# An mLSTM cell and a gelu feed-forward on one core: masks, two weight transfers, first states and idle products moved

## The chip, the cores and the metric

The kernel runs on one core of a Trainium2 chip. A core has TensorE (PE: products and, by a product with an identity, transposes), VectorE (DVE), ScalarE (ACT), GpSimd (POOL) and SyncE (SP), whose queue here issues every transfer. PEld is TensorE's loading of weights, which overlaps its products. The metric is the time of one execution in microseconds (us) on the device; lower is better.

## The reference

Two stages, all in float32. The first is an mLSTM cell over 4 batches, 8 heads, 768 steps and head size 40. It is a recurrence:

```python
for t in range(S):
    kt, vt, qt = (k[:, :, t], v[:, :, t], q[:, :, t])
    m_new = np.maximum(f_gate[:, :, t] + m, i_gate[:, :, t])
    f_stab = np.exp(f_gate[:, :, t] + m - m_new)
    i_stab = np.exp(i_gate[:, :, t] - m_new)
    m = m_new
    C = f_stab[:, :, None, None] * C + i_stab[:, :, None, None] * np.einsum('bhd,bhe->bhde', vt, kt)
    n = f_stab[:, :, None] * n + i_stab[:, :, None] * kt
    h_tilde = np.einsum('bhde,bhe->bhd', C, qt)
    nq = np.einsum('bhd,bhd->bh', n, qt)[:, :, None]
    denom = np.maximum(np.abs(nq), 1.0)
    o = 1.0 / (1.0 + np.exp(-o_gate[:, :, t]))
    y[:, :, t] = o * h_tilde / denom
```

The second stage takes the heads side by side as x (3072 tokens by 320) and computes

```python
h = x @ w_in                              # 320 x 2048
g = h * (1.0 / (1.0 + np.exp(-1.702 * h)))
return (g @ w_out).astype(np.float32)     # 2048 x 320
```

## The kernel before

The 768 steps are cut into six chunks `w` of 128 steps. A chunk is turned from a recurrence into products: scores of keys with queries, weighted by gates, times the values, plus what a carried state adds. Then the chunk's 512 tokens (4 batches of 128 steps) go through the feed-forward: up (320 to 2048), gelu, down (2048 to 320). While the feed-forward of chunk `w` runs on TensorE, the attention of chunk `w + 1` is laid in between its blocks.

Instructions stand on each engine in the order in which the program writes them; that order is made by hand. Tiles are taken from pools with a fixed number of buffers, and waits between engines come from who reads and writes which tile.

The first chunk has nothing to be laid beside, so it runs alone at the start. The parts that matter here:

- Transfers. SyncE issues, in this order: the gates of chunk 0; key and query of batch b for b = 0 to 3, with one weight piece behind each of b = 1, 2, 3; value and output gate of each batch; weight pieces 3 to 9. The weights are fetched as raw 32-bit pairs (two words per value) in pieces of 512 columns, and each piece is turned into the kernel's weight format by `convert` (L233 to L244): two operations of ScalarE, then four of VectorE. w_in has 320 rows: pieces of its first 128 and next 128 rows (`piece_in`, L132), and pieces 2 and 7 (`piece_rest`, L136) of the last 64 rows. A rest piece holds eight blocks of 128 columns, four in the upper and four in the lower 64 partitions, and `fetch` (L157) loads it with eight transfers of 64 KB.
- Idle products. `keep_busy(n)` (L186) issues n bf16 products of a tile of zeros into a PSUM bank that nothing reads. Eight stand at the start, four after `columns(0)`, two after each batch's values.
- Constants. After the identity, VectorE makes `pick`, then the masks `swap` and `keep` with the help of `odd` (L211 to L214), then `par`, `pair`, `half`. The masks are read only by `columns(w)` for w of 1 and more (L313, L314). Behind the constants in VectorE's queue stand the gates of chunk 0.
- `gates(0)` (L247): two scans along the steps and the sums around them on VectorE. GpSimd splits one of the results into three bf16 parts (`a3`, L261 to L264), VectorE another (`m3`, L272 to L275). They feed the products L367 and L368 in `weights(0, b)`, which build the exponents of the gate weights.
- For each batch: transposes of key and query (L338, copied out by ScalarE), scores (L387), weights (L363 to L368), with conversions of pieces 0 and 1 in between. Then for each batch tanh of the output gate (L731), values (L429), `outputs` on VectorE (L408 to L417) with a small copy of GpSimd (L420), idle products, and one batch later the `seam`: three transposes (L463) and a copy by ScalarE (L465), which put the batch's result into `xT`. The fourth seam stands alone at the end.
- The first feed-forward begins with `up(0, 0)` (L502): L512 multiplies the 256 first rows of w_in with `xT`, L518 the last 64. Between the blocks of `up` stand the products of the first carried state (`carry(0, c)`, L482, products at L490, copied to `state` by VectorE at L494) and conversions of the next pieces; after the fourth, `gates(1)` on VectorE.

Of the kernel before, what the change touches and what calls it, by code (L numbers as in the profile page):

```python
# [12 lines left out]
OP = mybir.AluOpType  # L13
AX = mybir.AxisListType
# [12 lines left out]
def kernel(  # L27
# [12 lines left out]
    nc = tc.nc  # L40
    B, H, S, D = q.shape
    BH = B * H
# [21 lines left out]
    op = ctx.enter_context(tc.tile_pool(name="op", bufs=2))  # L64
# [5 lines left out]
    V, A, G, T = nc.vector, nc.scalar, nc.gpsimd, nc.tensor  # L70
# [26 lines left out]
    def k_cols(w, t, h):  # L97

        return k_of(w)[t, h, :] if w < 2 else k_st[t, h * D:h * D + DP]
# [26 lines left out]
    rest_bits = w_in_bits[256:DM, :].rearrange("k (j two m) -> two k j m", two=2, m=256)  # L126
# [8 lines left out]

    def piece_rest(n):  # L136
        return (w_in_x[:, n * 4:n * 4 + 4, :].rearrange("p j m -> p (j m)"),
                [(slice(i * 64, i * 64 + 64), slice(j * 128, j * 128 + 128), rest_bits[i][:, n * 4 + j, :])
                 for i in range(2) for j in range(4)])

    def piece_out(n):
        parts, c = [], n * 512
# [12 lines left out]
    bits = {}  # L155

    def fetch(n):  # L157
        if n < 3 or 10 <= n < 13:
            bits[n] = s_in[:, n % 10].rearrange("p j m -> p (j m)").bitcast(U32).rearrange("p (a two) -> p a two", two=2)
        elif n == 17:  # L160
            bits[n] = t_flat[:, at_bits:at_bits + 1024].bitcast(U32).rearrange("p (a two) -> p a two", two=2)
        else:
            bits[n] = (gp if 6 <= n < 10 else sp).tile([128, 512, 2], U32, tag="g", name="bits")
        for r, c, src in pieces[n][1]:
            nc.sync.dma_start(out=bits[n][r, c].rearrange("p a two -> p (a two)"), in_=src)  # L165

    wt = {(0, b): gp.tile([L, NP, 2, L], FP, tag="g", name="wt") for b in range(B)}
    load_gates(0)
# [17 lines left out]
    def keep_busy(n):  # L186
        for _ in range(n):
            T.matmul(p_idle, idle, idle.unsqueeze(1).to_broadcast([128, 4, 128]), start=True, stop=True)
# [15 lines left out]
    for j in range(3):  # L204
        V.tensor_scalar(out=pick[j * BH:(j + 1) * BH, :], in0=ident[0:BH, 0:BH], scalar1=-1.0, scalar2=None,
                        op0=OP.mult)

    keep, swap = (const.tile([3 * BH, 3 * BH], FP, name=n) for n in ("keep", "swap"))
    odd = const.tile([3 * BH, 1], FP, name="odd")
    full = ident[0:3 * BH, 0:3 * BH]  # L210
    V.tensor_reduce(out=odd, in_=full.rearrange("p (j two) -> p two j", two=2)[:, 1], axis=AX.X, op=OP.add)  # L211
    V.tensor_scalar(out=swap, in0=full, scalar1=odd, scalar2=None, op0=OP.mult)
    V.memset(swap[BH:2 * BH, :], 0.0)
    V.tensor_tensor(out=keep, in0=full, in1=swap, op=OP.subtract)  # L214

    half = const.tile([BH, 2, 64], FP, name="half")
    par = const.tile([BH, 2], FP, name="par")
# [7 lines left out]
    state = [const.tile([128, BH // 2, D1], FP, name=f"state{i}") for i in range(2)]  # L225
# [76 lines left out]
    def slot(i, x):  # L302

        return slice((x ^ i) * HL, (x ^ i) * HL + HL)

    def banks(name):
        return ps_a.tile([128, 2, 512], FP, tag="a", name=name)

    def columns(w):
        pt = banks("p_cols")[:, 0, :]  # L310
        st = stacked[w]
        if w:
            T.matmul(pt[:, 0:3 * BH], st[0], keep, start=True, stop=False)  # L313
            T.matmul(pt[:, 0:3 * BH], st[1], swap, start=False, stop=True)  # L314
        else:
            T.transpose(pt[:, 0:3 * BH], st, full)
        n = 3 * BH
        if w in dec:
            n += BH
            T.matmul(pt[:, 3 * BH:n], half.rearrange("p a b -> p (a b)"), dec[w].rearrange("p a b -> p (a b)"),  # L320
                     start=True, stop=True)
        c = cols[w] = gate.tile([L, 4 * BH], FP, name="cols")
        V.tensor_copy(out=c[:, 0:BH], in_=pt[:, 0:BH])
        A.activation(out=c[:, BH:3 * BH], in_=pt[:, BH:3 * BH], func=AF.Exp, scale=-1.0)
        if w in dec:
            A.activation(out=c[:, 3 * BH:n], in_=pt[:, 3 * BH:n], func=AF.Exp)
# [130 lines left out]
    def seam(w, c, bs=(0, 1)):  # L457
        if w not in xT:
            xT[w] = work.tile([128, 3, B, L], FP, tag="xT", bufs=1, name="xT")
        px = banks("p_x")[:, 0:len(bs), 0:3 * L]  # L460
        for n, b in enumerate(bs):
            for x in range(3):
                T.transpose(px[:, n, x * L:(x + 1) * L], ys[w, c][:, b, x * 128:(x + 1) * 128], ident)  # L463
        b = 2 * c + bs[0]
        A.copy(out=xT[w][:, :, b:b + len(bs), :].rearrange("r x b t -> r b x t"),  # L465
               in_=px.rearrange("r b (x t) -> r b x t", t=L))
# [15 lines left out]
    def carry(w, c):  # L482
        js = slice(c * NJ, (c + 1) * NJ)
        pc = banks("p_c")
        n = 2 if 0 < w < NW - 1 else 1
        for j in range(NJ):
            for i in range(2):
                for x in range(n):
                    t = slot(i, x) if w else slice(0, L)
                    T.matmul(pc[i * 64:i * 64 + 64, x, j * D1:(j + 1) * D1], k_cols(w, t, c * PH + 2 * j + i),  # L490
                             vw[w, c][t, 2 * j + i, :], start=True, stop=True)
        new = lambda x: pc[:, x, 0:NJ * D1].rearrange("r (j d) -> r j d", d=D1)
        if w == 0:
            V.tensor_copy(out=state[1][:, js], in_=new(0))  # L494
            return
        for x, dst in enumerate((state_mid, state[1 - w % 2])[:n]):
            if x:
                decay(w, c, x, V)
            V.tensor_tensor(out=dst[:, js], in0=new(x), in1=dst[:, js], op=OP.add)
# [204 lines left out]
    def run(calls):  # L704
        for f, *args in calls:
            f(*args)
# [21 lines left out]
    for b in range(B + 1):  # L728
        if b < B:
            hs = slice(b * H, (b + 1) * H)  # L730
            A.activation(out=eo[0][:, hs, :], in_=eo[0][:, hs, :], func=AF.Tanh, scale=0.5)  # L731
            values(0, b)
            if b == 1:
                convert(2)
            keep_busy(2)
        if b:
            seam(0, (b - 1) // 2, ((b - 1) % 2,))


    beside = [((3, 4), (10, 11, 12, 13, 14)), ((5, 6, 7), (15,)), ((8, 9, 10), (16,)), ((11, 12, 13), (17, 18, 19)),  # L740
# [2 lines left out]
    def weights_in(n):  # L743
        for p in beside[n][0]:
            convert(p)
        for p in beside[n][1]:
            fetch(p)
# [8 lines left out]
    for w in range(NW):  # L756
        more = w + 1 < NW
        if w == 0:
            for j in range(NF // 2):
                if j % 2 == 0:  # L760
                    weights_in(j // 2)
                    up(w, j)
                if j == 0:
                    load(1, "o")
                if j < B:
                    (carry if j % 2 else scale)(0, j // 2)
                if j == 3:
                    gates(1)
                if j == 4:
                    load(1, "v")  # L770
                    spread(1)
                if j >= B:
                    transposes(1, j - B)
        else:
            token_sums(w)
            if more:
                gates(w + 1)
                load(w + 1, "o")
            for j in range(NF // 2):
                up_fast(w, j)  # L780
                if w == 1 and j < 4:
                    weight_sums(j)
                if more and j == 2:
                    load(w + 1, "vk")
                    spread(w + 1)
                if more and j:
                    for n in ((), (0, 2), (4,), (6, 1), (3,), (5, 7), ())[j - 1]:
                        block_transposes(w + 1, n)
                if j in (6, 7):
                    for late in (False, True):  # L790
                        hidden_sums(w, j - 6, late)
            gelu_fast(w, NF // 2 - 1)
            run([(hidden_sums, w, j, False) for j in (2, 3)])
        side = attention(w + 1) if more else {}
        if w == 0:

            blocks = [(lambda b=b, n=n: down(w, b, n)) for n0 in (0, 2) for b in range(B) for n in (n0, n0 + 1)]
        else:
            blocks = down_fast(w, 0) + down_fast(w, 1)
        for i, block in enumerate(blocks):  # L800
            if w == 0 and i < 6:
                weights_in(4 + i)
            if w + 2 < NW and i == (6 if w == 0 else 0):
                load_gates(w + 2)
            if w + 2 < NW and i == 13:
                load_squares(w + 2)
            block()
            run(side.get(i, []))
            if w and i == 0:
                run([(hidden_sums, w, j, True) for j in (2, 3)])  # L810
            if w == 0 and i in (11, 14):
                input_sums(slice(0, 4) if i == 11 else slice(4, 8))
# [30 lines left out]
```

## Time and profile before

| | us |
|---|---|
| median of 3 runs | 487.61 (487.58 to 489.2) |
| the profiled execution, its own time | 490.55 |
| its span, from first to last instruction | 488.8 |
| TensorE busy | 481.4 (98%) |
| VectorE busy | 344.8 (71%) |
| ScalarE busy | 194.6 (40%) |
| GpSimd busy | 149.9 (31%) |
| first product of the first feed-forward (L512) | starts at 35.27 |
| SyncE's transfers of the first rest piece | 10.18 to 18.24 |

Times inside the profile count from the span's start. In a list in order of time, a line has the start, the time from the first start to the last end of a group, the engine, the source line, the operation, the tiles (written <- read), shapes, a count, and in brackets the idle time of the engine just before it with what ended it. SPq is SyncE's queue; its times are those of issuing. A wait for several things is put down to the one that came last. The granted clock is the share of TensorE's full clock that the throttle allowed.

### The profile page before, as it was taken

The page shows a single profiled execution, that of the slowest core. Times are in us where ns is not written, and L with a number is a line of the kernel's source. Part 1 is how long each engine was busy: PE and PEld are TensorE (multiplying, and loading weights), DVE is VectorE, ACT ScalarE, POOL GpSimd, SP SyncE. Part 2 cuts the span into 40 slices and gives each one's busy share as a digit, 9 for nine tenths or more (in the row PEclk, how much of TensorE's full clock was granted, in tenths as well). Part 3 has the DMA queues.
Part 4 walks back from the last instruction along what each step waited for, and adds up shares of the span by engine and source line. Part 5 has one row for each costly group of instructions (what it writes and reads, how often), then busy time and mean ns, then how long its engine had stood idle before and what let it go on. Part 6 is the DMA issues. An engine that isn't in the chain of part 4 may idle for free.

```text
span 488.8 us, 12119 instructions
## 1 busy us (share of the span) xinstructions
PE 481.4 (98%) x5011; PEld 389.1 (80%) x5011; DVE 344.8 (71%) x682; ACT 194.6 (40%) x432; POOL 149.9 (31%) x145
## 2 busy tenths in 40 slices
PE   8989999999999999999999999999999999999997
PEld 5774446777777999877999876999876999876997
DVE  6663796989768968667978577978577957353812
ACT  3644656901344720254620264630164640164200
POOL 6020001600198630036630045640035640035300
PEclk9988999999999999999999999999999999999999
DMA  8699997001994000799000699000599100000000
GB/s 175 137 246 178 261 203 160 32 16 46 213 169 83 2 30 4 141 186 164 5 30 4 125 197 166 9 30 4 115 198 163 18 30 3 28 0 1 0 28 27
DMA packets 130982, 44.31 MB, mean 91 GB/s; under 512 B 105808, under 2 KB 128368, under 8 KB 130928
## 3 DMA queue, kind: packets, MB, share of 16 engines
q1 hardware_dynamic: 130928, 43.55, 48.3%
q8 instruction: 39, 0.64, 0.6%
q14 instruction: 15, 0.12, 0.1%
HBM read 39.52 MB, written 4.01 MB: 89 GB/s over the span
## 4 chain that ended last, share of the span: by engine, by line
PE 92%; SPq 5%; DMA 1%; DVE 1%; issue 0%; ACT 0%; DVEq 0%
PE p_out L684 32%; PE p_h L582 26%; PE p_h L587 8%; PE p_out L633 7%; PE p_h L512 6%; PE p_c L490 2%; SPq L165 2%; SPq L121 2%; PE p_o L439 2%; PE p_s L398 2%; PE p_i L447 2%; PE p_h L518 2%; PE p_x L463 2%; DMA bits<-in_moe_w_in_dram 1%; PE p_t L338 1%
## 5 line engine op out<-in xcount | busy, mean ns | idle before, releaser
L624 POOL TENSOR_TENSOR g<-g,parts 128x512 f32<-128x512 f32 x30 | 38.3, 1277 | 124.4 <-DVE parts L616 113.3
L684 PE MATMUL p_out<-w_out_sb,g 128*128 128x160 f32 x480 | 71.0, 302 | 0.0
L684 PEld LDWEIGHTS p_out<-w_out_sb,g 128*128 128x128 f32 x480 | 66.6, 190 | 0.9
L582 PE MATMUL p_h<-xT,w_in_sb 128*128 128x256 f32 x240 | 67.0, 388 | 0.0
L563 ACT ACTIVATE g<-g 128x512 f32<-128x512 f32 x80 | 50.0, 631 | 35.6 <-DVE g L619 25.2
L582 PEld LDWEIGHTS p_h<-xT,w_in_sb 128*128 128x128 f32 x240 | 43.8, 190 | 20.2 <-issue 7.6
L465 ACT COPY xT<-p_x 128x768 f32<-128x768 f32 (+1 forms) x14 | 9.9, 707 | 113.6 <-PE p_x L463 113.6
L689 DVE TENSOR_TENSOR o_sb<-o_sb,p_out 128x160 f32<-128x160 f32 x70 | 21.0, 316 | 43.8 <-PE p_out L684 43.4
L684 PE MATMUL p_out<-t_sb,s 128*128 128x160 f32 x320 | 47.2, 301 | 0.0
L684 PEld LDWEIGHTS p_out<-t_sb,s 128*128 128x128 f32 x320 | 44.4, 190 | 0.2
L615 DVE TENSOR_TENSOR t_x<-p_h,parts 128x256 f32<-128x256 f32 x40 | 16.7, 418 | 39.2 <-PE p_h L587 34.6
L582 PE MATMUL p_h<-t_x,s_in 128*128 128x256 f32 x160 | 41.1, 379 | 0.0
L587 PE MATMUL p_h<-xT,w_in_x 64*128 64x512 f32 x160 | 39.8, 615 | 0.0
L374 ACT ACTIVATE wt<-wt,cols 128x64 f32<-128x64 f32 x160 | 38.8, 338 | 0.0
L420 POOL COPY y<-y 128x128 f32<-128x128 f32 (+1 forms) x14 | 4.0, 285 | 108.4 <-DVE y L417 108.4
L633 PE MATMUL p_out<-w_out_sb,g 128*128 128x320 f32 x128 | 36.3, 437 | 0.0
L582 PEld LDWEIGHTS p_h<-t_x,s_in 128*128 128x128 f32 x160 | 30.4, 190 | 4.1
L612 ACT COPY parts<-p_h 128x256 f32<-128x256 f32 x40 | 15.0, 374 | 45.9 <-PE p_h L582 45.9
L512 PE MATMUL p_h<-xT,w_in_sb 128*128 128x512 f32 x64 | 32.1, 647 | 0.6 <-ACT xT L465 0.6
L633 PEld LDWEIGHTS p_out<-w_out_sb,g 128*128 128x128 f32 x128 | 23.6, 190 | 9.2 <-DVE w_out_sb L244 0.3
L616 DVE TENSOR_TENSOR parts<-p_h,t_x 128x512 f32<-128x512 f32 x40 | 27.7, 692 | 4.2
L623 ACT COPY g<-p_h 128x512 f32<-128x512 f32 x30 | 17.4, 580 | 30.6 <-PE p_h L587 25.2
(192 smaller groups left out, 898.5 us busy)
## 6 DMA issues: line engine op xcount, KB each, us to landing
wt<-m_row SPq DMA_DIRECT2D x40, 128.0 KB, 4.4
k_sq<-in_k_dram SPq DMA_DIRECT2D x16, 320.0 KB, 5.6
q_sq<-in_q_dram SPq DMA_DIRECT2D x16, 320.0 KB, 10.0
out_dram<-o_sb SPq DMA_DIRECT2D x24, 160.0 KB, 1.8
eo<-in_o_gate_dram SPq DMA_DIRECT2D x5, 640.0 KB, 9.9
bits<-in_moe_w_in_dram SPq DMA_DIRECT2D x6, 512.0 KB, 5.9
v_st<-in_v_dram SPq DMA_DIRECT2D x14, 160.0 KB, 5.0
bits<-in_moe_w_out_dram SPq DMA_DIRECT2D x6, 320.0 KB, 4.6
```

The lines of the kernel that those rows point to most:

```text
L374: A.activation(out=x[:, h, :], in_=x[:, h, :], func=AF.Exp, scale=-1.0, bias=cols[w][:, c * PH + h:c * PH + h + 1])
L512: T.matmul(ph[j][i], w_in_sb[:, c, f * 128:(f + 1) * 128], x[:, c, :], start=(first and c == 0), stop=(not first and c == 1))
L563: A.activation(out=gs[w, j][:, i, :], in_=gs[w, j][:, i, :], func=AF.Gelu_apprx_sigmoid)
L582: T.matmul(out, a, x[n], start=start, stop=stop)
L587: T.matmul(row, w_in_x[r, j, :], rest_x[r, 2, :], start=not late, stop=late)
L615: V.tensor_tensor(out=u2, in0=both[:, 1, right], in1=y[:, left], op=OP.add)
L616: V.tensor_tensor(out=y[:, half_w:3 * half_w].rearrange("p (a t) -> p a t", a=2), in0=flat[:, half_w:3 * half_w].rearrange("p (a t) -> p a ...
L623: A.copy(out=g[:, 0, :], in_=row0)
L624: G.tensor_tensor(out=g0, in0=g0, in1=u, op=OP.add)
L633: T.matmul(po, gs[w, f // 2][:, f % 2, b * L:(b + 1) * L], w_out_sb[:, f, :], start=(f == 0), stop=(f == NF - 1))
L684: T.matmul(po, a(f), b[:, f, :], start=(f == 0), stop=(f == NH - 1))
L689: V.tensor_tensor(out=dst, in0=x, in1=po, op=OP.add)
```

## The change

Five edits. The masks' four VectorE operations move, as a function `masks()`, from the constants to behind `gates(1)` in the first feed-forward. A rest piece is fetched with two transfers (one for each 64 partitions, four runs of 128 columns each) instead of eight. The first states are copied out of PSUM by ScalarE instead of VectorE. Three idle products are added ahead of the fourth seam, and two after it.

```diff
     def piece_rest(n):
         return (w_in_x[:, n * 4:n * 4 + 4, :].rearrange("p j m -> p (j m)"),
-                [(slice(i * 64, i * 64 + 64), slice(j * 128, j * 128 + 128), rest_bits[i][:, n * 4 + j, :])
-                 for i in range(2) for j in range(4)])
+                [(slice(i * 64, i * 64 + 64), None, rest_bits[i][:, n * 4:n * 4 + 4, :]) for i in range(2)])
...
         for r, c, src in pieces[n][1]:
-            nc.sync.dma_start(out=bits[n][r, c].rearrange("p a two -> p (a two)"), in_=src)
+            to = bits[n][r].rearrange("p a two -> p (a two)")
+            to = to.rearrange("p (j m) -> p j m", m=256) if c is None else to[:, 2 * c.start:2 * c.stop]
+            nc.sync.dma_start(out=to, in_=src)
...
-    V.tensor_reduce(out=odd, in_=full.rearrange("p (j two) -> p two j", two=2)[:, 1], axis=AX.X, op=OP.add)
-    V.tensor_scalar(out=swap, in0=full, scalar1=odd, scalar2=None, op0=OP.mult)
-    V.memset(swap[BH:2 * BH, :], 0.0)
-    V.tensor_tensor(out=keep, in0=full, in1=swap, op=OP.subtract)
...
+    def masks():
+        V.tensor_reduce(out=odd, in_=full.rearrange("p (j two) -> p two j", two=2)[:, 1], axis=AX.X, op=OP.add)
+        V.tensor_scalar(out=swap, in0=full, scalar1=odd, scalar2=None, op0=OP.mult)
+        V.memset(swap[BH:2 * BH, :], 0.0)
+        V.tensor_tensor(out=keep, in0=full, in1=swap, op=OP.subtract)
...
         if w == 0:
-            V.tensor_copy(out=state[1][:, js], in_=new(0))
+            A.copy(out=state[1][:, js], in_=new(0))
             return
...
             if b == 1:
                 convert(2)
             keep_busy(2)
+        if b == B:
+            keep_busy(3)
         if b:
             seam(0, (b - 1) // 2, ((b - 1) % 2,))
+    keep_busy(2)
...
                 if j == 3:
                     gates(1)
+                    masks()
```

## The prediction

> **What bounds the kernel now.** I read the page first, then the chain that ended last, then the engines in order of time over the first 62 us, and last the granted clock in short stretches. The chain's shares are TensorE's:
>
> ```profile
> PE 92%; SPq 5%; DMA 1%; DVE 1%; issue 0%; ACT 0%; DVEq 0%
> ```
>
> From 35.27 us to the last product at 485.6 us the chain is one unbroken row of products, so a change can gain there only where it removes products. This one removes none. All its edits act before the first product of the feed-forward part (L512 at 35.27 us), or on engines that stand beside TensorE. Inside the first 35 us, TensorE in order of time, with the idle time before an instruction in brackets:
>
> ```profile
> 7.90 0.23 PE L368 MATMUL p_w<-t_sb 96*128 96x128 bf16 x1 [0.43 <-POOL t_sb L262]
> ...
> 20.91 1.16 PE L387 MATMUL p_s<-qT,kT 40*128 40x128 f32 x14 [0.54 <-DVE wt L389]
> ...
> 31.79 0.60 PE L188 MATMUL p_idle<-t_sb 128*128 128x512 bf16 x2
> 32.43 0.53 PE L463 MATMUL p_x<-ident,y 128*128 128x128 f32 x3
> 33.82 0.88 PE L463 MATMUL p_x<-ident,y 128*128 128x128 f32 x3 [0.86 <-DVE y L417]
> 35.27 6.25 PE L512 MATMUL p_h<-xT,w_in_sb 128*128 128x512 f32 x8 [0.57 <-ACT xT L465]
> 41.45 1.99 PE L518 MATMUL p_h<-xT,w_in_x 64*128 64x512 f32 x8
> 43.37 3.70 PE L512 MATMUL p_h<-xT,w_in_sb 128*128 128x512 f32 x8
> ```
>
> Two things: from 7.90 us TensorE is nearly gapless up to 32.4, so what lets L368 start at 7.90 sets everything after it. And the same eight L512 take 6.25 us at 35.27 and 3.70 at 43.37. The busy time of each engine in short stretches says why; the last three numbers are granted clock, DMA share and GB/s:
>
> ```profile
> 33.20:33.60 0.40, 0.00 (x0) 0.00 (x0) 0.40 (x1) 0.28 (x1) 0.00 (x0) 1.00 1.07 210
> 33.60:34.00 0.40, 0.18 (x1) 0.21 (x2) 0.08 (x1) 0.00 (x0) 0.26 (x2) 0.51 1.05 223
> ...
> 40.20:40.40 0.20, 0.20 (x1) 0.00 (x0) 0.09 (x1) 0.00 (x0) 0.00 (x0) 0.50 0.74 246
> 40.40:40.60 0.20, 0.20 (x2) 0.10 (x1) 0.17 (x1) 0.00 (x0) 0.00 (x0) 0.91 1.19 451
> ```
>
> The clock is halved from about 33.62 to 40.45, 6.83 us.
>
> **What the Trainium skill says.** TensorE: Matmul & The Clock Gate, Part 1: an activity monitor halves the clock after an idle window of about 3.4 us and restores it after a busy one; windows run free of the kernel, so the phase differs by run. The trace agrees on half speed and on length (6.83 = 2 x 3.41), not on the trigger: the window 30.2 to 33.6 was busy for about 2.7 of 3.4 us and still cost the clock. The same page, Part 2, Step-by-step: products run in program order; so a product of nothing ahead of a waiting transpose delays it if it is still running. SBUF — State Buffer, Who interferes with whom: a VectorE copy in a two-port mode and a GpSimd operation exclude each other for a whole instruction. The trace agrees: the small copy L221 lasted 0.80 us, to 3.94, beside GpSimd's memset of q_sq, which ended at 3.87.
>
> **Part by part.** Masks. VectorE and GpSimd at the start:
>
> ```profile
> 1.98 0.20 DVE L211 TENSOR_REDUCE odd<-ident 96x1 f32<-96x48 f32 x1
> 2.94 0.17 DVE L219 TENSOR_REDUCE par<-ident 32x2 f32<-32x32 f32 x1
> 3.14 0.73 POOL L223 MEMSET q_sq<- 128x768 f32 x1
> 3.14 0.80 DVE L221 COPY half<-par 32x128 f32<-32x128 f32 x1
> 4.54 0.42 POOL L261 CAST room<-room 32x128 bf16<-32x128 f32 x1 [0.68 <-DVE room L259]
> ```
>
> The four mask operations hold VectorE from 1.98 to 2.94: 0.96 us ahead of the gate scans. Without them L221 comes at about 2.2, ahead of the long memsets; the gates land at 0.80 + 1.7 = 2.5 and 1.26 + 1.7 = 2.96 us, so L255 can start near 3.05 instead of 4.00 and L259 end near 3.6 instead of 4.48. GpSimd's chain L261 to L262, which releases L368, can then start when its memset ends, 3.87 instead of 4.54: 0.67 at most. The other input of the products, VectorE's L273, ended at 7.20 and moves by more. TensorE's key and query transposes end at 6.63 and do not bind; the second batch's query lands at 3.43 + 4.3 = 7.7, before its transposes at 8.3. Bounds: 0 if L221 again loses the port to the memset, 0.75 if the memset too gets done earlier. I take 0.6 us, and it carries through: down to L512 TensorE, ScalarE and VectorE wait only for each other (the data of v and the gates come far sooner, next paragraph). The masks themselves cost about 0.9 us of VectorE after the second chunk's gates near 60 us and are read at 82.2 us: hidden by 20 us; bare, they would cost 0.9.
>
> Transfers. SyncE's queue in order of time:
>
> ```profile
> 10.18 8.06 SPq L165 DMA_DIRECT2D s_in<-in_moe_w_in_dram  x8
> 18.28 0.59 SPq L121 DMA_DIRECT2D v_st<-in_v_dram  x1
> ...
> 24.93 12.90 SPq L165 DMA_DIRECT2D bits<-in_moe_w_in_dram  x14
> ```
>
> Eight issues become two, twice. The six removed cost about 0.6 each, and those at 10.18 and 13.19 took 2.34 and 1.85, so v and o move 3.6 to 6.5 us ahead and what follows piece 7 about 3.6 more. Who waited for them? Only ScalarE, 0.3 us, for o of the second batch; VectorE uses that tanh later than it is made. The first v product at 23.0 follows the idle products, not v. Gain on the path 0; lower bound 0 too, since k and q of all batches stand ahead in the queue.
>
> First states by ScalarE. VectorE waited 9.7 us in all at L494 for two carry products, with the conversions of pieces 5 to 7 and gates(1) behind it. Now ScalarE waits: behind it there stand its halves of the conversions (L237, L238) and the gelus. Each copy is about 0.45 us (L465, 128x384, took 0.48). Pieces 5 to 7 start about 0.7 us later on VectorE (end 56.4 instead of 55.7); the product that reads piece 7 starts at 62: cover 5.6 us. ScalarE idles 1.75 us ahead of the next gelu, more than the wait plus the copy (about 1.0). gates(1) come about 2.5 us earlier. TensorE waits for none of it: 0; if the cover were gone, 0.7 twice.
>
> Products of nothing. Three between the third and fourth seam, two after the fourth. Warm, one takes about 0.21 us (eight at the cold start stand 0.43 apart): three from 32.96 end at 33.6, before y of the fourth batch at 33.68; two from 34.3 end at 34.75, before xT at about 34.8. Cost 0 warm; cold 5 x 0.43, of which about 0.6 stands out. Their bank is p_idle's own, so no buffer waits are added. What they can gain is the cold stretch: 6.25 - 3.63 = 2.62 on the first eight products, 0.89 - 0.49 = 0.40 on the fourth seam, 3.0 in all. Counting the columns that TensorE streams, the window that lost the clock had about 0.36 of full rate, the least busy that kept it 0.39. With 3 x 0.21 more it has 0.55, and windows of other phases 0.5 or more. I expect the clock to hold.
>
> Sum against the profiled execution: 490.55 - 3.0 - 0.6 = **486.9 us** (span 485.2). Against the median of 487.61 this is only 0.7. The runs shown are 487.58, 487.61, 489.2 and the profiled 490.55. A full cold window of products costs 3.41 / 2 = 1.7, two of them here 3.0: the four fit 0, 0, 1.6 and 3.0 above 487.6. So I read the median as a warm run, from which the products of nothing have nothing to take, and the gain as the 0.6 us of the masks.
>
> **Rivals.** (1) The median run is cold too, and the profiled one is longer for reasons of its own. For it: two runs at one value fit one whole cold window as well as none, and by my count most phases touch the threshold. Then 487.6 - 1.7 - 0.6 = 485.3, or with two windows 484.0. Against: TensorE's row after 35 us leaves no place for 1.3 to 2.9 us of profiling cost. (2) The masks' time isn't on the path: GpSimd's chain or the port binds, 487.5. (3) Slower: the clock falls anyway and the five products stand in the way at half speed. For it: the threshold (between 0.36 and 0.39) is worked out from one trace. Price: 487.0 warm + 3.0 + 0.6 = 490.5, with its place at the fourth seam; it decides once the clock falls before 33.6 in the median run. (4) One cold window stays: 488.5.
>
> **How the numbers follow.** Half a per cent, about what a measurement of this kernel can tell from no change, is 2.44 us: below 485.17 or above 490.05. Chances: forecast 0.54 (its own range 486.4 to 487.4), rival 1 0.30 (one window 0.18, two 0.12), rival 2 0.08, rival 3 0.04, rival 4 0.04. Faster: the 0.12 and, as 485.3 lies at the bound, 0.08 of the 0.18; slower: rival 3 and 0.01 of what I haven't seen; the rest same. The range 485.0 to 487.8 leaves out the 0.12 and the 0.08 of rivals 3 and 4.
>
> **What would show it.** Right: L368 at about 7.3 instead of 7.90; first L512 near 34.2 with eight of them in about 3.7 us; granted clock 1.00 from 8 us on; v issued before 15 us; L494 on ScalarE and no wait of TensorE near 60 us. Wrong: a halved clock near 33 to 40, L221 again near 0.8 us, or a seam that starts only after its idle products. If times below 485.2 come with a span whose first L512 is near 34.2, the runs of before were cold.

## The result, and the profile after

| | before | after |
|---|---|---|
| median of ten runs beside each other (us) | 488.38 | 486.68 |
| lowest to highest (us) | 487.57 to 490.54 | 486.64 to 486.81 |
| after over before (95% interval) | | 0.9963 (0.9948 to 0.9978) |
| the profiled execution (us) | 490.55 | 486.67 |
| its span (us) | 488.8 | 485.0 |
| first product of the first feed-forward (us) | L512 at 35.27 | L515 at 34.09 |

The kernel is 0.37% faster, which is within the half per cent called no change. The forecast was 486.9. To understand the numbers one has to know that runs of before fall into levels, at 487.6 and at 1.6, 2.95 and 4.6 us above it, by how many windows of TensorE's clock (stretches of 3.41 us) were halved in them: their mean granted clock is 1.00, 0.996, 0.992 and 0.989. A run with a halved window is called cold below. The ten runs stand five at 487.6, four at 489.15 and one at 490.54, so their median lies between two levels. Against the level without a halved clock the gain is 487.59 - 486.68 = 0.91 us; the rest of the gap of the two medians is clock that before loses and after keeps.

The line numbers moved by three in most places: L371 is the old L368, L515 the old L512, L521 the old L518, L466 the old L463, L420 the old L417, L189 the old L188, L497 the old L494, L218 the old L221, L258 and L259 the old L261 and L262. The chain that ended last, shares by engine:

```profile
PE 95%; DVE 3%; POOL 1%; ACT 0%; issue 0%; POOLq 0%; DVEq 0%
```

SyncE's queue, which held 5% of the chain before, is gone from it. The sooner transfers gained 0.09 us at most by themselves (experiment 3), so a share of the chain is not yet time that can be gained.

TensorE in order of time:

```profile
7.07 0.23 PE L371 MATMUL p_w<-t_sb 96*128 96x128 bf16 x1 [0.43 <-POOL t_sb L259]
...
20.07 1.16 PE L390 MATMUL p_s<-qT,kT 40*128 40x128 f32 x14 [0.55 <-DVE wt L392]
...
31.96 0.81 PE L189 MATMUL p_idle<-t_sb 128*128 128x512 bf16 x3
32.99 0.54 PE L466 MATMUL p_x<-ident,y 128*128 128x128 f32 x3 [0.21 <-DVE y L420]
33.36 0.59 PE L189 MATMUL p_idle<-t_sb 128*128 128x512 bf16 x2
34.09 3.70 PE L515 MATMUL p_h<-xT,w_in_sb 128*128 128x512 f32 x8
37.72 1.99 PE L521 MATMUL p_h<-xT,w_in_x 64*128 64x512 f32 x8
```

L371 starts 0.83 us earlier than L368 did, and the 0.83 is carried to the scores (20.91 to 20.07) and to the fourth seam (33.82 to 32.99). The wait ahead of that seam, 0.86 before, is now three idle products and 0.21. L521 starts at 37.72 instead of 41.45, 3.73 us earlier: 0.83 from the start, 0.35 from the seam (35.27 - 34.09 = 1.18, less 0.83), and 2.55 from the first eight products (6.18 from first start to the start of L521, now 3.63). Two of the short stretches that the prediction shows of before, now in the changed kernel:

```profile
33.60:34.00 0.40, 0.35 (x2) 0.00 (x0) 0.00 (x0) 0.40 (x2) 0.40 (x1) 1.00 0.94 205
...
40.20:40.40 0.20, 0.20 (x2) 0.16 (x1) 0.09 (x1) 0.00 (x0) 0.00 (x0) 1.00 1.29 129
```

The granted clock, third number from the end, stays at 1.00 where it stood at 0.51 and 0.50. The start, VectorE and GpSimd:

```profile
2.19 0.34 DVE L218 COPY half<-par 32x128 f32<-32x128 f32 x1
...
3.15 0.73 POOL L220 MEMSET q_sq<- 128x768 f32 x1
...
3.84 0.29 POOL L258 CAST room<-room 32x128 bf16<-32x128 f32 x1
```

`half` is written at 2.19 in 0.34 us, ahead of the long memsets, instead of 0.80 beside one. GpSimd's first cast starts as its memset ends, at 3.84 instead of 4.54, and takes 0.29 instead of 0.42. SyncE's queue and ScalarE's copy of the first state:

```profile
10.30 2.74 SPq L166 DMA_DIRECT2D s_in<-in_moe_w_in_dram  x2
13.09 0.61 SPq L121 DMA_DIRECT2D v_st<-in_v_dram  x1
...
21.86 5.31 SPq L166 DMA_DIRECT2D bits<-in_moe_w_in_dram  x8
```

```profile
44.45 0.43 ACT L497 COPY state<-p_c 128x328 f32<-128x328 f32 x1 [0.48 <-PE p_c L493]
```

The rest piece takes 2.74 us of the queue instead of 8.06, v is issued at 13.09 instead of 18.28, and the issue of pieces 3 to 9 is done at 27.2 instead of 37.8. ScalarE waits 0.48 us, copies in 0.43, and still idles 0.83 ahead of its next gelu.

### The profile page after: what moved, and what is told of

Its sections match the earlier page's. It is cut to its first block, busy times and chain, and to the rows that moved or that the text cites. A ratio compares the mean times of both kernels' runs of the same rounds, so it can differ in the third digit from the quotient of the medians.

```text
span 485.0 us, 12103 instructions
## 1 busy us (share of the span) xinstructions
PE 479.3 (99%) x5016; PEld 388.0 (80%) x5016; DVE 344.0 (71%) x680; ACT 195.3 (40%) x434; POOL 149.7 (31%) x145
## 4 chain that ended last, share of the span: by engine, by line
PE 95%; DVE 3%; POOL 1%; ACT 0%; issue 0%; POOLq 0%; DVEq 0%
PE p_out L687 32%; PE p_h L585 26%; PE p_h L590 8%; PE p_out L636 7%; PE p_h L515 6%; PE p_c L493 3%; PE p_o L442 2%; PE p_s L401 2%; PE p_i L450 2%; PE p_h L521 2%; PE p_x L466 1%; PE p_t L341 1%; PE p_o L432 1%; PE p_s L390 0%; DVE wt L392 0%
## 5 line engine op out<-in xcount | busy, mean ns | idle before, releaser
L515 PE MATMUL p_h<-xT,w_in_sb 128*128 128x512 f32 x64 | 29.5, 604 | 0.1
```

The lines of the kernel that those rows point to most:

```text
L515: T.matmul(ph[j][i], w_in_sb[:, c, f * 128:(f + 1) * 128], x[:, c, :], start=(first and c == 0), stop=(not first and c == 1))
```

## The experiments

My theory after the result: the masks give their time in every run; the five products give nothing to a run whose clock holds and take away the halved windows; transfers and first states give nothing. Rivals: that it isn't the products that hold the clock, and that the masks' time is given back later. The lengths of a gap or a gain are read from traces, the levels from times. Runs of before beside these experiments, 171 in all, stood 87 at 487.6, 27 at 489.2, 26 at 490.5 and 31 at 492.2: half of them lost clock.

**1 to 3: each part alone.** The first kernel is before with the masks moved.

```diff
-    V.tensor_reduce(out=odd, in_=full.rearrange("p (j two) -> p two j", two=2)[:, 1], axis=AX.X, op=OP.add)
...
+    def masks():
...
                     gates(1)
+                    masks()
```

> The kernel before with the masks moved and nothing else. My theory (the masks set the start of the gate products; the idle products take away cold clock windows only): the start of L368's products moves from 7.90 to about 7.1 us and every run loses 0.8, so runs with a warm clock stand at 486.75; about half of the runs still stand 1.6 or 3.0 above that. Rival (the value transfers that come sooner moved the first 35 us, not the masks): 487.6 at the lowest.

The second is before with the five idle products.

```diff
+        if b == B:
+            keep_busy(3)
         if b:
             seam(0, (b - 1) // 2, ((b - 1) % 2,))
+    keep_busy(2)
```

> The kernel before with the five idle products and nothing else. My theory: no run is cold any more, all runs within 0.3 of 487.55, clock 1.00, L368 at 7.90 as before. Rival 1 of the prediction (the 487.6 runs of before were cold too): 485.9 or less. Rival 3 (the products stand in the way): some runs at 490 and more.

The third is before with the two transfers and the first states by ScalarE.

```diff
+                [(slice(i * 64, i * 64 + 64), None, rest_bits[i][:, n * 4:n * 4 + 4, :]) for i in range(2)])
...
-            V.tensor_copy(out=state[1][:, js], in_=new(0))
+            A.copy(out=state[1][:, js], in_=new(0))
```

> The kernel before with two transfers for a rest piece and the first states by ScalarE. My theory: neither is on the path, so the lowest run is 487.6 and the spread to 489.2 and 490.5 stays. Rival (sooner transfers gain): lowest run at 486.8. Rival (ScalarE's wait costs): lowest run at 488.0 or more.

| | runs | at full clock | other runs | ratio to before (95% interval) |
|---|---|---|---|---|
| masks | 22 | 18 at 486.75 | 4, from 488.43 to 489.71 | 0.9958 (0.9938 to 0.9978) |
| products | 22 | 14 at 487.59 | 8, from 489.09 to 489.45 | 0.9968 (0.9948 to 0.9988) |
| transfers, states | 22 | 14 at 487.5 | 3 at 489.1, 2 at 490.5, 3 at 492.1 | 0.9985 (0.9962 to 1.0009) |

At full clock the parts add up: masks 0.84, transfers and states 0.09 at most, products 0.00, together 0.93 against the 0.91 measured. TensorE of the kernel with the masks alone, at full clock, starts its first feed-forward where the changed kernel does, with a wait of 0.85 us and no idle product:

```profile
32.98 0.54 PE L465 MATMUL p_x<-ident,y 128*128 128x128 f32 x3 [0.85 <-DVE y L419]
34.08 3.70 PE L514 MATMUL p_h<-xT,w_in_sb 128*128 128x512 f32 x8 [0.57 <-ACT xT L467]
```

The profiled run of the third kernel shows one halved window at the seam, by the clock from 34.67 to 38.08 us, and the first eight products are 5.25 us long:

```profile
34.92 5.25 PE L513 MATMUL p_h<-xT,w_in_sb 128*128 128x512 f32 x8 [0.57 <-ACT xT L466]
```

What I missed is in the clock. The products didn't end all lost windows: 8 of 22 runs still lost one. And the masks, which put nothing on TensorE, thinned them out too: 4 of 22, where half of before's are cold and I had expected about half. The level at 4.6 us, 31 of 171 runs of before, is in neither kernel. That suggests two places: one that the products close, and one that the masks close, with 1.6 + 2.95 = 4.55 us where both strike. The levels don't prove it. The two places are not independent, since 58 runs with the 1.6 and 57 with the 2.95 among 171 would meet in 19 runs by chance and do in 31; and a 1.6 can be lost at the seam too, as the third kernel's profiled run (489.05) shows. The second place can't be the seam, whose wait is as long with the masks moved (0.85 us) as before (0.86). New theory: it is the start, where TensorE waits for the gates between 5 and 8 us.

**4: six and four idle products instead of three and two,** in the changed kernel.

```diff
-            keep_busy(3)
+            keep_busy(6)
...
-    keep_busy(2)
+    keep_busy(4)
```

> The changed kernel with twice the idle products, six and four. My theory: three and two just fill their waits, so the further five (0.21 each) stand out: the fourth seam starts about 0.5 later, the first L512 about 0.6 later in all, 487.3 in every run. Rival (the waits have room left): 486.7.

486.91 to 487.37 in 18 of 22 runs, 487.88 to 488.47 in the other four; median 487.1, 0.4 us more than with three and two. The seam comes behind its idle products, 0.26 us later than in the changed kernel, and L515 starts 0.35 us later:

```profile
31.96 1.46 PE L189 MATMUL p_idle<-t_sb 128*128 128x512 bf16 x6
33.25 0.49 PE L466 MATMUL p_x<-ident,y 128*128 128x128 f32 x3
...
34.44 3.60 PE L515 MATMUL p_h<-xT,w_in_sb 128*128 128x512 f32 x8
```

So the price of an idle product is its 0.21 us less the gap it fills. Three are about what fits the 0.86 us; the gaps had more room left than I thought, 0.35 us lost where I had said 0.6. More products don't steady the clock further: two of the four long runs have a span 1.3 and 1.6 us longer than the rest, at a mean clock of 0.998 and 0.999, which is less than a whole lost window (0.996); what they lost, and where, no trace shows.

**5: the start made longer.** Before with the five products, and the four mask operations written twice where they stood.

```diff
+    V.tensor_reduce(out=odd, in_=full.rearrange("p (j two) -> p two j", two=2)[:, 1], axis=AX.X, op=OP.add)
+    V.tensor_scalar(out=swap, in0=full, scalar1=odd, scalar2=None, op0=OP.mult)
+    V.memset(swap[BH:2 * BH, :], 0.0)
+    V.tensor_tensor(out=keep, in0=full, in1=swap, op=OP.subtract)
```

> The kernel before with the five idle products and with the four mask operations written twice ahead of the gates. Theory: of the products alone, 8 of 22 runs stood 1.6 above the rest with a mean clock of 0.996, though nothing at the fourth seam waits any more. I now think that a second cold window can come at the start: TensorE waits for the gates between 5 and 8 us, and a window that ends near 8.5 finds it idle. Then a longer wait makes it commoner: warm runs at 488.3 (0.96 less what GpSimd's memset hid), over half of the runs 1.6 above, and a profile of such a run has the halved clock from 7 to 10 us on, not at 33. Rival (the cold window of those runs lies between 27 and 33 us, where the value products are short): the share of cold runs stays at about a third, and a cold profile shows it there.

Four of 22 runs at 488.7 (I had said 488.3), and 18 cold: nine at 490.4, three near 491.5, six at 493.1. At full clock it costs 1.15 us. The profiled run is one of the 490.4, and its clock is halved at the start, not at the seam:

```profile
6.04:9.46 3.42, 1.40 (x14) 0.90 (x15) 3.17 (x11) 1.07 (x2) 2.98 (x9) 1.00 1.06 245
9.46:12.87 3.41, 3.41 (x22) 2.80 (x21) 0.40 (x1) 1.30 (x3) 1.51 (x5) 0.50 0.95 228
```

TensorE was busy for 1.40 of 3.42 us, while it waited for VectorE and GpSimd to make the gates' parts, and the next window ran at half speed. The longer wait took the cold share from 8 to 18 of 22. Nine of the 18 lost more than one window (mean clock 0.990 to 0.993), although the five products stand at the seam; no trace of such a run was kept, so where they lost the others stays open.

**6: the start filled.** The same as experiment 2, and three idle products more between the first transposes and the products with the gates; the masks stay in front.

```diff
         for b in range(B):
...
+        if b == 0:
+            keep_busy(3)
```

> The kernel before with the five idle products, and with three more between the first batch's transposes and its gate products, masks where they were. Theory of the cold window at the start: the wait is filled, so the third of runs at 489.2 is gone and all stand at 487.6. Rival (cold window between 27 and 33 us, or masks alone matter): a third of the runs stays 1.6 above.

```profile
6.26 0.81 PE L188 MATMUL p_idle<-t_sb 128*128 128x512 bf16 x3
...
7.91 0.23 PE L368 MATMUL p_w<-t_sb 96*128 96x128 bf16 x1 [0.43 <-POOL t_sb L262]
```

L368 still starts at 7.91: the products lie in the wait. Of 22 runs 19 are between 487.56 and 487.87, the others 488.10, 488.13 and 488.81; all have the same span (485.9 or 486.0) and a mean clock of 0.999 or 1.00, and none stands at the 489.1 to 489.45 that 8 of 22 had without them. So the start is the second place, shown from both sides. Moving the masks closes it by shortening a wait of TensorE that nothing else fills: with the masks moved and the products in place none of 51 runs is cold (the changed kernel and experiments 7, 8 and 11). It is not what the idle products of the change do.

**7: the changed kernel without the two products behind the seam.**

```diff
-    keep_busy(2)
```

> The changed kernel without the two products behind the fourth seam. By the count of streamed columns: a window that ends near 33.5 is helped, one that ends near 35 has 0.33 to 0.45 of full rate and stands at the threshold. Warm runs 486.7; a few runs, up to a quarter, 1.6 above. Rival (three are enough): all at 486.7.

486.66, 486.62 to 486.77 in 18 runs, none cold, where I had allowed for up to a quarter; ratio to before 0.9943 (0.9923 to 0.9962). L515 starts at 34.08 behind a wait of 0.57 us. The two products do nothing that can be measured here; three, with the masks out of the way, are enough.

**8 and 11: the wait of the seam itself.** The chain of the changed kernel runs through VectorE from 26.2 to 32.9: outputs of group 1, the conversion of piece 2, outputs of groups 2 and 3. In 8 that conversion stands behind the values of group 3.

```diff
-            if b == 1:
+            if b == 3:
                 convert(2)
```

> The changed kernel with the conversion of piece 2 emitted beside the fourth batch's values instead of the second's. The chain after the change runs through VectorE from the second batch's outputs to the fourth, 2.4 of it this conversion; but the fourth batch's values end at 31.13 and its outputs start at 31.37, so only about 0.25 is to be had: 486.4. Rival (the conversion is then late for L521 at 37.7): 486.7 or more.

486.61 (486.58 to 486.87, 17 runs), 0.07 less than the changed kernel and not the quarter expected. VectorE's last outputs start 0.22 us earlier (31.15 instead of 31.37), but GpSimd's small copy of y behind them now meets VectorE's conversion. The engines of run 8 in order of time:

```profile
32.56 0.42 DVE L236 TENSOR_SCALAR w_in_x<-w_in_x 128x512 f32<-128x512 f32 x1
...
32.70 0.37 POOL L423 COPY y<-y 128x64 f32<-128x64 f32 x1 [2.24 <-DVE y L420]
```

In the changed kernel the copy took 0.24 us. The third transpose of the seam reads it. Run 11 tests this: the conversion behind the fourth seam, with nothing on VectorE beside the copy, and without the last two products.

```diff
-            if b == 1:
-                convert(2)
...
-    keep_busy(2)
+    convert(2)
```

> The changed kernel with the conversion of piece 2 behind the fourth seam, so that VectorE has nothing queued behind the last outputs while GpSimd copies the last columns of y, and without the last two idle products. If the small gain of the late conversion (0.06 us) was kept down by GpSimd's copy of y, which took 0.37 us beside VectorE's conversion instead of 0.24, the fourth seam comes 0.13 us earlier than with the late conversion: 486.45 to 486.5. If the copy had no part in it: 486.6. If the later conversion makes the second weights late, 487 or more, with TensorE waiting ahead of an L515 for VectorE's halves near 45 us.

```profile
32.81 0.54 PE L466 MATMUL p_x<-ident,y 128*128 128x128 f32 x3 [0.26 <-DVE y L420]
33.91 3.70 PE L515 MATMUL p_h<-xT,w_in_sb 128*128 128x512 f32 x8 [0.57 <-ACT xT L468]
37.81 1.99 PE L521 MATMUL p_h<-xT,w_in_x 64*128 64x512 f32 x8 [0.20 <-DVE w_in_x L241]
```

The copy is back at 0.24 us and L515 starts at 33.91, 0.11 earlier than in run 8 and 0.18 earlier than in the changed kernel. But L521 needs piece 2 at 37.6 and VectorE is done with it 0.2 late, so the time is 486.75 (486.72 to 486.79). So the copy is slow only where it stands beside VectorE's conversion (in run 8 it ends at 33.07, 0.09 behind that operation's end at 32.98). The seam's 0.2 us can't be had by moving this conversion to either place. The late weights came at the first L521 and not, as I had written, near 45 us.

**9, 10 and 12: fewer idle products.** With the conversion late, TensorE's own queue should set the time from 21 us on, so that the idle products of before now cost what they take. Run 9 is run 8 without the four ahead of the values; run 10 has besides one instead of two behind each group of values; run 12 is run 8 with two instead of the four.

```diff
     columns(0)
-    keep_busy(4)
...
-            keep_busy(2)
+            keep_busy(1)
```

> The changed kernel with the conversion of piece 2 behind the values of group 3 and without the four idle products between the transposed columns and the values of group 0 (21.30 to 22.16 in the changed kernel's trace, 0.86 us on TensorE). Theory that in this order TensorE's own queue sets the time from 21 us to the fourth seam: 0.8 us faster than the changed kernel, 485.8, first L515 near 33.2. Rival that the four hold the clock: some runs go cold by one window or two, at 487.4 or above. Rival that the outputs on VectorE set the time even with the conversion moved: 486.6, no gain.

> The kernel of the run before this one with one idle product instead of two behind each of the four groups of values (four fewer, 0.21 us each). Theory that TensorE's queue still sets the time: up to 0.64 us less (three of the four lie ahead of the last outputs), 485.2, all at full clock. Rival that VectorE's and GpSimd's outputs end last at the seam by now: within 0.1 of the run before it. Rival that so few products lose the clock: several runs 1.5 us or more above the fastest.

> The changed kernel with the conversion of piece 2 behind the values of group 3 and with two idle products instead of four ahead of the values of group 0. If the loss of the clock without the four was a matter of how much TensorE streams in the 3.4 us around them, two of them (0.43 us less on TensorE's queue) leave some phases below the point: warm runs at 486.15 to 486.2, and fewer cold ones than the half without any, between none and a third, at 489 or more. Rival that any two products are enough, wherever they stand: all runs at 486.2. Rival that the start decides and not these products: no cold run, as with all four.

| | runs | at full clock | cold runs | mean of all |
|---|---|---|---|---|
| 8, all of them | 17 | 17 at 486.61 | none | 486.63 |
| 12, two of the four | 14 | 13 at 486.2 | 495.07 | 486.83 |
| 9, none of the four | 6 | 3 at 485.81 | 493.19, 494.71, 494.72 | 490.01 |
| 10, and one for two | 6 | 1 at 485.12 | 490.55 to 492.55, five | 490.28 |

The gains at full clock are about those worked out: 0.43, 0.80, and 0.69 more (one run only, 0.64 expected). That run 10 would keep its clock was wrong. The losses are 5.4 to 8.9 us; the profiled run of 10 lost 7.2 us in five windows. TensorE of run 10, cold, first in order of time and then by windows of its clock:

```profile
21.31 2.50 PE L432 MATMUL p_o<-v_st,wt 128*128 128x41 f32 x16
...
24.04 3.47 PE L432 MATMUL p_o<-v_st,wt 128*128 128x41 f32 x16
```

```profile
19.01:22.42 3.41, 2.87 (x31) 2.51 (x28) 2.90 (x6) 1.08 (x2) 0.00 (x0) 1.00 1.13 179
22.42:25.83 3.41, 3.41 (x19) 3.32 (x18) 1.49 (x7) 0.94 (x3) 0.24 (x1) 0.50 1.09 208
25.83:29.25 3.42, 3.42 (x17) 3.22 (x18) 1.38 (x5) 0.64 (x2) 0.16 (x1) 0.50 0.98 339
```

TensorE is busy for 2.87 of 3.41 us and loses the clock; then it is busy without a gap and doesn't get it back, window after window, until 39.48. What runs there are values products, 41 columns wide, on 128 x 128 weights each. Run 12 has the best median of all and not the best mean: its one cold run in fourteen costs 8.9 us, more than the 0.43 saved in thirteen, though one such run says little of how often they come. Between the changed kernel and run 8 the difference is 0.07 us; no version here beats the changed kernel by an amount that matters.

## Why the prediction was right, and where it was not

486.9 was said and 486.68 measured, with the span at 485.0 instead of 485.2. Point by point:

- **Masks, 0.6.** Right mechanism, mis-sized: 0.83, above the bound of 0.75. The step that failed is "GpSimd's chain L261 to L262 ... can start when its memset ends, 3.87 instead of 4.54: 0.67 at most". It started at 3.84, 0.70 earlier, and its cast was also 0.13 shorter (0.29 for 0.42): the two make up the 0.83. The 0.13 is time that the cast had lost beside VectorE's scan. In before it overlaps the scan L265 (4.41 to 4.88) and ends at 4.96; in experiment 7, where that scan is over at 3.84 as the cast starts, it takes 0.28, and VectorE's next cast beside it 0.33 instead of 0.21. I had the Trainium skill's SBUF — State Buffer, Who interferes with whom, in hand and used it for VectorE's copy alone; by the same lock GpSimd's cast can be the one that is held up. The traces agree with that as far as they go: they show the overlap and the lost time, not the lock. It carried through whole, and the second rival (0, 487.5) falls. At 55.69 to 56.67 us the masks delay VectorE by 0.9 us and no product waits for it.
- **Transfers and first states, 0.** Right on the path. They gave 0.09 us at most; from the first L515 on, the changed kernel is ahead of the kernel with the masks alone by 0.07 us in the times and 0.04 at the end of the traces, and where that comes from I have not found. The transfers of v and o are issued 2.8 to 5.2 us sooner, where 3.6 to 6.5 was said. L497 waits and copies for 0.91 us (about 1.0 predicted), and `gates(1)` start at 52.55 instead of 58.84; less the 3.73 us by which everything moved, that is 2.6 us, where 2.5 was said.
- **Products of nothing, 0 at full clock and 3.0 on a cold stretch.** Right: 487.59 against 487.6 at full clock (experiment 2), and 2.55 + 0.35 = 2.90 between the two profiled executions. Price and fit of an idle product too (experiment 4). Two of the five do nothing (experiment 7).
- **The clock will hold, by streamed columns per window.** The outcome was right, in part by luck, and the reasoning too small. I looked at one seam; there were two places. The step "Counting the columns that TensorE streams, the window that lost the clock had about 0.36 of full rate, the least busy that kept it 0.39" came from one execution, in which the window at the start happened to keep its clock. Experiments 2, 5 and 6 show that in other executions it doesn't. It was the masks, counted as 0.6 us of waiting and nothing else, that closed it. With the products alone, from which I expected no cold run, 8 of 22 were.
- **The median is a warm run.** 487.61 was one, and so the likeliest case stood; rival 1 (485.3 or 484.0) falls. But that was the luck of three runs: half of the 171 are cold, and the ten beside the changed kernel have a median of 488.38, so that the two medians stand 1.70 us apart and not the 0.7 that was said. The levels 0, 1.6 and 3.0 read from four runs were right; the fourth, 4.6, wasn't in them.
- **Rivals 3 and 4** (490.5, and one window left, 488.5) fall: none of the changed kernel's ten runs lost a window, nor any of the 41 runs of experiments 7, 8 and 11, which keep its masks and the three products.

What would show it came as said: L371 at 7.07, L515 at 34.09 with eight in 3.70, clock 1.00, the first v before 15 us, L497 on ScalarE, no wait of TensorE near 60.

## What to carry to other kernels

Where the time of a kernel falls into levels, look up the granted clock before reading a median, and look for every stretch in which TensorE waits: a wait of TensorE that is shortened by moving work on another engine can be worth clock as well as time (here 0.8 us in every run, and 1.6 us more in the third of the runs that lost a window there). Fill a gap of TensorE with idle products up to the length of the gap and no further, and judge the taking away of such products by many runs and their mean, since the saving shows in each run and the loss only in some. When an operation moves, look at what stands beside it on GpSimd and VectorE before and after, and count what each had lost to the other.

## What the runs showed of the hardware

- **Busy in the profile is not what the clock goes by.** The Trainium skill, TensorE: Matmul & The Clock Gate, Part 1, has the clock halved after an idle window of about 3.4 us and restored after a busy one. The length agrees in every trace with a halved clock (3.41 us, a lost one costing 1.4 to 1.6 us here). The trigger doesn't. The first of these two windows (before) lost the clock with TensorE busy for 2.73 us, and the second (experiment 3) was followed by full clock with 2.00:

```profile
30.20:33.62 3.42, 2.73 (x22) 2.04 (x20) 3.21 (x11) 1.33 (x3) 0.23 (x1) 1.00 0.99 332
...
3.95:7.37 3.42, 2.00 (x12) 1.00 (x10) 3.12 (x12) 0.93 (x2) 2.51 (x7) 1.00 1.05 185
```

In run 10 a window with 2.87 us lost it, and four windows in a row, busy to the full, did not bring it back.

- **A count of columns does better; it is an estimate, and not shown.** Let a product count its columns, about 0.42 ns each at full clock and 0.83 at half (idle products of 512 columns stand 0.22 and 0.43 us apart), twice for float32 (eight L515 of 512 columns take 3.63 us), and take that times the share of the 128 rows that it uses. In the fourteen traces shown or used here, the four windows that lost the clock come to 0.25 (experiment 5), 0.28 (run 10), 0.35 (experiment 3) and 0.36 (before) of their length, and all that kept it to 0.39 or more. At half clock, five that stayed there come to 0.33 or less, and those that got it back to 0.40 or more. This is the prediction's count with its 0.36 and 0.39, but for the rows: without them run 10's window, in which scores of 40 rows run, comes to 0.63 and doesn't fit. The rows were put in with the outcome known, and no run was made to test them.
- **Products of zeros hold the clock.** Three of them at the start took the cold runs from 8 of 22 to none of 22 (experiments 2 and 6); without the four ahead of the values 3 of 6 runs were cold, with them none of 17 (runs 9 and 8).
- **GpSimd's short operations stretch too**: the copy of y from 0.24 to 0.37 us beside VectorE's conversion (run 8) and the cast L261 from 0.28 to 0.42 beside VectorE's scan, as VectorE's copy of `half` did from 0.34 to 0.80 beside a memset.
